# Window attention and a two-layer network on one core: value loads released one tile ahead of key and query loads, attention blocks moved among the products

## The chip, the cores and the metric

The kernel runs on one core of one Trainium2 chip. The core has five engines with instruction queues of their own: PE (TensorE, matrix products), DVE (VectorE), ACT (ScalarE), POOL (GpSimd) and SP (SyncE, which here only issues DMAs). Each executes its own queue in order; engines wait for each other, and for DMAs, through semaphores. The metric is the device time of one execution in microseconds. A profiled execution gives a span (first to last instruction) besides.

## The reference

Attention with a window of 128 positions and 4 sink positions, over q, k, v of shape (4 batches, 8 heads, 768 positions, 64); the heads are then put side by side as x of shape (4, 768, 512), which passes through a normalisation, a layer to 2048 with ReLU, a layer back to 512, and a residual:

```python
scores = scale * np.matmul(q, k.transpose(0, 1, 3, 2))
keep = is_sink | in_window                 # position < 4, or 0 <= row - column < 128
scores = np.where(keep, scores, -1000000000.0)
a = np.exp(scores - np.max(scores, axis=-1, keepdims=True))
a = a / (np.sum(a, axis=-1, keepdims=True) + 1e-09)
x = np.matmul(a, v)                        # then heads to the last axis: (4, 768, 512)
xn = (x - mu) / np.sqrt(var + 1e-06) * g_ln
out = x + np.maximum(xn @ w_ch1, 0.0) @ w_ch2
```

Inputs and output are float32; products run in bf16.

## The kernel before

**Tiles and chunks.** 3072 rows are 24 tiles of 128 rows; two tiles are a chunk, so there are 12 chunks, three to a batch. Weights stay in SBUF. In names, a number after a letter group is a tile or a chunk: `sc16` is the score block of tile 16, `ph6_0` the first product of chunk 6.

**What happens to a chunk** from chunk 4 on (chunks 0 to 3 get their keys and queries transposed by TensorE instead):

1. POOL issues four loads of keys and queries (`kld`, `qld`, L722; float32 in memory, bf16 in SBUF, 128 KB each in bf16) and six or seven loads of values (`vld`, L664, into a ring of seven buffers `vn`). `load_m` cuts the values into half blocks, because the 64-row halves of the windows lie differently for heads 0 to 3 and 4 to 7.
2. SP issues a transposing DMA for each loaded half (`trk`, `trq`, L595), giving kT and qT.
3. `block(t)` makes one block of matmuls, `sc{t}`, that holds the values product of tile t−1 (L976, L983, L992: probabilities times values) and the scores of tile t (L1003), and for an even tile the sink scores of the chunk (L1011). ScalarE takes the exponential (`ex`, L1021), VectorE applies the band mask (`mk`, L1026).
4. VectorE divides the values product of tile t−1 by the sums (`rc` and `x`, L1044 and L1046, one for each half of the heads), takes mean and variance (`bn`, `ag`, L900 and L902); POOL takes the power −1/2 (`rs`, L910 and L911); VectorE makes the normalised tile (`xc`, L914); SP issues the transposing DMA `trx` into xnt (L595 again).
5. `mlp(c)` multiplies xnt of the chunk (both tiles) with the first weights in eight products `ph{c}_0` to `ph{c}_7` (L1062, eight matmuls of 128x256 each); ScalarE or VectorE takes the ReLU (`rl`, L1073 and L1075). The second layer is, for chunks 3 to 10, a product by seven half-size products `P1` to `P7` (L1113, eight matmuls each; `k1`, `k6`, `k5` and `o12` copy from PSUM, L1119; `o11`, `o22`, `o21` add, L1123); for the others it is sixteen matmuls of 128x512 for each tile (`pc`, L1167). The residual is added (`o`, L1150 or L1175), and SP issues the store (`st`).

While TensorE does the products of one chunk, it does the score blocks of the next chunk between them: of a chunk's two blocks, `sc{2c}` and `sc{2c+1}`, each stands at a place among the products of chunk c−1 or its predecessor.

**What sets the order.** Every operation is recorded with a priority, its engine or engines, a cost, and its dependencies. `Plan.run` plays them through a small cost model and writes out one order for each engine; that order is then fixed in the program. Operations with two possible engines (ReLUs, copies) go to the one that the plan finds first free. The priority of a block is `at(c, "blk") + step * i - lead`, so `step` is the distance in priority between a chunk's two blocks and `lead` how far ahead of the default a chunk's blocks stand (`PAR["lead"]`, the last entry holding for all chunks from 5 on). A DMA has a triple for the plan: time on the shared line, delay before, delay after. `SHARED` is the time until which the plan counts transfers of both kinds of queue as one line; after it, each kind counts as a line of its own. None of these figures is in the program; the order that they lead to is.

**The gates.** `gate(c)` and `gate_v(c)` add a dependency to a chunk's key and query loads and to its value loads: they wait for `rs` of an earlier tile. A transposition of queries also waits for `trx` of tile 2c−3. POOL and SP issue in order, so a load that waits holds up what stands behind it.

PSUM has eight banks: four in two `pair` buffers for scores, four `one` buffers for everything else (two halves of a values product, `ph`, `P`).

Of the kernel before, what the change touches and what calls it, by code (L numbers as in the profile page):

```python
# [65 lines left out]
class Plan:  # L66
# [4 lines left out]
    PE_DRAIN = 0.18  # L71
    SWITCH = 0.095
    LANES = 8
    SHARED = 62.0

    def __init__(self):
        self.ops = []
# [36 lines left out]
    def run(self):  # L114
# [8 lines left out]
        while ready:  # L123
# [4 lines left out]
            for o in ready:  # L128
                if "PE" in o.engs and o is not head and o.prio >= PAR["strict"]:
                    continue  # L130
# [43 lines left out]
            else:  # L174
                busy, first, last = o.dma
                q = "POOL" if e == "POOL" else "HW"
                at = max(st + occ + first, dma_free[q], dma_free["all"] if st < self.SHARED else 0.0) + busy
                dma_free[q] = dma_free["all"] = at
# [18 lines left out]
def pe(us):  # L197
    return {"PE": (us, us + Plan.PE_DRAIN)}
# [7 lines left out]
def dve(n, per=1.04):  # L206
    t = 0.067 + 0.001 * per * n
    return (t, t + 0.09)


def fix(occ, extra=0.09):
    return (occ, occ + extra)


SW = (0.9, 0.7, 0.9)
# [2 lines left out]
SW_W = (2.65, 0.7, 0.9)  # L218
HW_F = (0.8, 2.2, 0.5)
HW_S = (0.75, 0.8, 1.2)  # L220
HW_X = (1.0, -0.2, 0.6)
SW_2 = (0.65, 0.7, 0.9)
HW_T = (0.10, 0.8, 0.8)
SW_H = (0.45, 0.7, 0.9)
SW_Q = (0.25, 0.7, 0.9)

LOW, HIGH = 1e-9, 1e9
LAST_CUTS, LAST_ACT = (0, 320, 512), (3,)
# [2 lines left out]
NEVER = -1e9  # L231
BIG = 3.3e38

PAR = dict(strict=400.0, win=0.4, tr=-8.0, sc=-5.0, sc1=-2.0, av=2.0, blk=-8.0, step=8.0, trx=9.0, by_dma=4, x_by_dma=2,
           w1p=(1.6, 2.6, 2.7, 2.8), pm=3, w2p=(4.5, 4.51, 4.52, 4.53), apart=2, vs0=(2.0, 13.0), by_tile=0, vp=(0.0, 0.1, 2.0, 2.1, 4.55, 4.56), ld1=0.05, t0=0.8, warm=7.9, pm0=-40.0, w1g=17.0, gtt=1.25, seven=3, lead=(0, 0, 0, 2, 4, 6), w2t=-4.0, at7=(0.5, 1.5, 2.5, 3.5, 4.5, 6.5, 7.5))


def general(tc, nc, slots, pairs, ones, ident_f, ident, w1, w2, mhalf, g_s, g_r, q, k, v, out, scale):
# [133 lines left out]
def kernel(  # L372
# [24 lines left out]
    NC = B * RC  # L397
# [70 lines left out]
    def constant(name, eng, us, prio, emit, reads=(), **kw):  # L468
        return P.op(name, {eng: fix(us)}, prio, emit, reads=[Bc[r] for r in reads], **kw)

    V, G = nc.vector, nc.gpsimd
# [44 lines left out]
    def negs(e):  # L516
# [27 lines left out]
    for b in range(B):  # L544
        n_vs = 4 if b else H
        P.op(f"vs{b}", {"DVE": dve(260)} if b else {"POOL": (0.9, 1.0)}, PAR["vs0"][0] if b == 0 else 48.0 * b - 20, lambda e, b=b, n=n_vs: (V if b else G).tensor_tensor(
            vs[b], vc[:, b, :].unsqueeze(1).to_broadcast([128, n, 65]),
            (sel4 if b else sel).unsqueeze(2).to_broadcast([128, n, 65]), op=ALU.mult),
            reads=[Bc["vcd"], Bc["vc"], Bc["sel4" if b else "sel"]], writes=[Bvs[b]], nb=PAR["vs0"][1] if b == 0 else 40.0 * b)

# [7 lines left out]
    for c in range(4):  # L558
        for n in range(len(Bw1[c])):
# [3 lines left out]
                 writes=[Bw1[c][n]], dma=half_w if len(Bw1[c]) > 1 else SW_W)  # L563
    for c in range(4):
        P.op(f"w2ld{c}", {"POOL": (0.75, 0.8)}, PAR["w2p"][c], lambda e, c=c: G.dma_start(
            w2[c], moe_w_ch2[512 * c:512 * (c + 1), :].rearrange("(t p) n -> p t n", p=128)),
            writes=[Bw2[c]], dma=SW_W)
# [17 lines left out]
    rs_op, trx_op = {}, {}  # L585
    natf_users, natp_users = [], []

    def gate(c):
        return [rs_op[2 * c - (4 if c > 5 else 5)]] if PAR["by_dma"] < c < NC else []

    def gate_v(c):
        return [rs_op[2 * c - (3 if c == 5 else 4)]] if PAR["by_dma"] < c <= NC else []

    def dma_t(dst, src):
        nc.sync.dma_start_transpose(out=dst, in_=src)  # L595
# [54 lines left out]
    def load_m(t, prio):  # L650
# [12 lines left out]
        for i, (p0, n, hs, src) in enumerate(parts):  # L663
            P.op(f"vld{t}_{i}", {"POOL": (0.8, 0.85)}, prio + 0.001 * i, lambda e, p0=p0, n=n, hs=hs, src=src: G.dma_start(  # L664
                m.t[p0:p0 + n, hs, 0:64], src), writes=[m], dma=SW_H if n == 128 else SW_Q, after=list(ones_of.values()) + gate_v(t // 2))

# [5 lines left out]
    def chunk(c):  # L672
# [3 lines left out]
        if c < 2:  # L676
            kT_b[c], qT_b[c] = Buf(f"kT{c}", "kT"), Buf(f"qT{c}", "qT")
            if c == 0:
                nats = [Buf("kf", "natf"), Buf("qf", "natf")]
                for hh in range(2):  # L680
                    hs = slice(4 * hh, 4 * hh + 4)
                    for i, (x, T) in enumerate(((k, kT_b[c]), (q, qT_b[c]))):
                        nm, src, part = "kq"[i], nats[i], Buf(f"{'kq'[i]}l{hh}")
                        ap = x[b, hs, 0:256, :].rearrange("h (p i) d -> p h (i d)", i=2)
# [3 lines left out]
                        nat, pt, done = Buf(f"{nm}c{hh}", "natc"), Buf(f"pt{nm}{hh}", "one"), Buf(f"{nm}T0{hh}")  # L688
                        natf_users.append(P.op(f"cast{nm}{hh}", {"DVE": dve(512), "ACT": act(512)}, d + 0.01 * hh,
                             lambda e, nat=nat, src=src, hs=hs: (nc.scalar.copy if e == "ACT" else V.tensor_copy)(  # L690
                                 nat.t, src.t[:, hs].rearrange("p h i d -> p i h d")),
# [18 lines left out]
        else:  # L710
            both = []
            for nm, src, bT in (("k", k, kT_b), ("q", q, qT_b)):
                T = Buf(f"{nm}T{c}", nm + "T")
                bT[c] = T
                if c < PAR["by_dma"]:
                    both.append((nm, src, T, ld + (0.1 if nm == "q" else 0.0)))
                    continue
                for i in range(2):
                    nat = Buf(f"{nm}n{c}{i}", "nat")
                    ap = src[b, :, 256 * R + 128 * i:256 * R + 128 * (i + 1), :].rearrange("h p d -> p h d")  # L720
                    P.op(f"{nm}ld{c}{i}", {"POOL": (0.87, 0.9)}, ld + 0.01 * i + (0.1 if nm == "q" else 0.0),
                         lambda e, nat=nat, ap=ap: G.dma_start(nat.t, ap), writes=[nat], dma=SW, after=gate(c))  # L722
                    P.op(f"tr{nm}{c}{i}", {"SP": (1.2, 1.2)}, d + 0.01 * i, lambda e, T=T, nat=nat, i=i: dma_t(
                        T.t[:, :, 128 * i:128 * i + 128], nat.t.rearrange("p h d -> p (h d)")),
                        reads=[nat], writes=[T], dma=HW_X, after=[trx_op[2 * c - 3]] if c > PAR["by_dma"] and nm == "q" else [])
            if both:
# [170 lines left out]
    def normalise(c, i, d, st, x, xc):  # L897
# [25 lines left out]
        if c >= PAR["x_by_dma"]:  # L923
            trx_op[t] = P.op(f"trx{t}", {"SP": (1.2, 1.2)}, d + 0.5, lambda e: dma_t(xnt_b[c].t[:, :, 128 * i:128 * i + 128], xc.t),
                 reads=[xc], writes=[xnt_b[c]], dma=HW_X)
            return
# [257 lines left out]
    for c in range(NC):  # L1184
        chunk(c)
        if c < 2:
            attend_tile(2 * c)
            attend_tile(2 * c + 1)
        elif c < RC:
            attend(c)  # L1190
        else:
            block(2 * c)
            block(2 * c + 1)
# [5 lines left out]
    w2t = [[flat_f[0][:, m] for m in range(2)], [flat_f[1][:, m] for m in range(2)], flat_p[0:2], flat_p[2:4]]  # L1199
# [21 lines left out]
    def guard(e):  # L1221
# [92 lines left out]
```

## Time and profile before

| | |
|---|---|
| time, three runs | 212.18, 213.89 and 215.04 us; median 213.89 us |
| profiled execution, time | 212.65 us |
| its span | 211.1 us |
| TensorE busy in the span | 202.0 us |
| VectorE, ScalarE, POOL busy | 156.8, 116.0, 114.3 us |
| bytes moved by DMAs | 28.06 MB |
| queue of POOL's DMAs, queue of SP's DMAs: time of their packets, share of 16 engines' span | 91.3%, 38.1% |

Lines of the profile name the engine, the line of the kernel, the operation, what is written from what is read (buffer numbers left out), a count, busy or elapsed time, and the idle time of the engine just before with what ended it. Issuing a DMA is no busy time of SP; a DMA's issue and its landing are different moments. A wait for several semaphores is put down to the one that came last by the profile. PEclk, the clock granted to TensorE, is full speed in the whole span. The profile is of one execution.

### The profile page before, as it was taken

How to read it: one execution, taken by the hardware profiler on the slowest of the kernel's cores; microseconds unless marked ns; L12 is line 12 of the kernel's file. 1: busy time of each engine (PE TensorE's matmuls, PEld its weight loads, DVE VectorE, ACT ScalarE, POOL GpSimd, SP SyncE). 2: the span in 40 equal slices, each digit the busy share in tenths (PEclk: the TensorE clock that was granted, in tenths of full speed). 3: DMA queues.
4: the chain of work that ended last, by engine and by line, in shares of the span. 5: the costliest groups of instructions: out<-in, count | busy, mean ns of one | idle time of the engine just before them, and what ended most of it. 6: DMA issues, size and time to landing. Idle time of an engine off the chain costs nothing.

```text
span 211.1 us, 7043 instructions
## 1 busy us (share of the span) xinstructions
PE 202.0 (96%) x2891; PEld 161.2 (76%) x2891; DVE 156.8 (74%) x426; ACT 116.0 (55%) x200; POOL 114.3 (54%) x169
## 2 busy tenths in 40 slices
PE   7799999999989998998999999999999999999994
PEld 2458865755865887886888888887888888888853
DVE  5599877999766489789688799788797788891321
ACT  4798697285662473564474564563563563454510
POOL 7969842479837972981970991972961321030000
PEclk9999999999999999999999999999999999999999
DMA  5999999999999999999999799899999520310203
GB/s 158 188 187 200 190 207 198 171 174 143 151 198 162 132 145 133 82 148 187 82 142 181 66 169 180 90 147 169 115 200 89 112 56 1 127 26 3 99 0 109
DMA packets 105644, 28.06 MB, mean 133 GB/s; under 512 B 94852, under 2 KB 102664, under 8 KB 105608
## 3 DMA queue, kind: packets, MB, share of 16 engines
q0 software_dynamic: 70960, 13.18, 91.3%
q1 hardware_dynamic: 33448, 13.71, 38.1%
q10 hardware_dynamic: 1200, 0.69, 1.2%
q8 instruction: 23, 0.38, 0.7%
q14 instruction: 13, 0.11, 0.2%
HBM read 27.43 MB, written 6.29 MB: 160 GB/s over the span
## 4 chain that ended last, share of the span: by engine, by line
PE 74%; DMA 12%; DVE 9%; ACT 2%; POOL 1%; issue 1%; ACTq 0%; DVEq 0%
PE one L1062 33%; PE one L1113 17%; PE one L1167 13%; DMA xnt<-xc 6%; DMA qT<-nat 3%; DMA natf<-in_q_dram 3%; DVE st L900 2%; PE pair L1003 2%; PE one L976 2%; PE one L983 1%; DVE x L1046 1%; PE one L992 1%; PE pair L1011 1%; ACT qT L669 1%; POOL st L911 1%
## 5 line engine op out<-in xcount | busy, mean ns | idle before, releaser
L1062 PE MATMUL one<-xnt,w 128*128 128x256 bf16 x768 | 89.8, 273 | 2.1 <-DMA xnt<-xc 1.1
L1062 PEld LDWEIGHTS <-w 128*128 128x128 bf16 x768 | 73.5, 98 | 13.6 <-DMA xnt<-xc 2.3
L1073 ACT ACTIVATE h<-one 128x512 bf16<-128x512 f32 x87 | 52.0, 598 | 40.1 <-PE one L1062 39.0
L664 POOL DMA_DIRECT2D vn<-in_v_dram x59 | 39.4, 695 | 8.4 <-DMA w<-in_moe_w_ch_dram 7.1
L1021 ACT ACTIVATE pe<-pair 128x768 bf16<-128x768 f32 x36 | 27.3, 808 | 22.7 <-PE pair L1003 22.3
L910 POOL TENSOR_SCALAR st<-st 128x1 f32<-128x1 f32 x24 | 9.3, 388 | 56.0 <-DVE st L902 55.3
L1167 PE MATMUL one<-w,h 128*128 128x512 bf16 (+2 forms) x144 | 29.5, 356 | 0.1
L1167 PEld LDWEIGHTS <-h 128*128 128x128 bf16 x144 | 13.4, 98 | 12.3 <-DMA w<-in_moe_w_ch_dram 0.4
L1113 PEld LDWEIGHTS <-h 128*128 128x128 bf16 x192 | 18.8, 98 | 2.5 <-issue 0.2
L911 POOL TENSOR_TENSOR st<-st,mhalf 128x1 f32<-128x1 f32 x24 | 16.5, 688 | 2.0
L900 DVE BATCH_NORM_STATS2 st<-x 128x6 f32<-128x512 bf16 x24 | 16.6, 693 | 0.7
L1113 PE MATMUL one<-w,h 128*128 128x256 bf16 x128 | 16.6, 273 | 0.1
L1113 PEld LDWEIGHTS <-sb 128*128 128x128 bf16 x156 | 15.0, 98 | 1.9
L722 POOL DMA_DIRECT2D nat<-in_k_dram x16 | 15.0, 938 | 2.2 <-DMA natp<-in_q_dram 1.5
L1046 DVE TENSOR_TENSOR x<-one,rec 128x256 bf16<-128x256 f32 x36 | 15.2, 422 | 0.9
L1123 DVE TENSOR_TENSOR ot<-one,tx 128x256 f32<-128x256 f32 x24 | 9.5, 420 | 7.5 <-PE one L1113 4.9
L1175 DVE SCALAR_TENSOR_TENSOR ot<-one,st,x 128x512 f32<-128x512 f32 (+2 forms) x9 | 6.2, 691 | 11.6 <-PE one L1167 10.3
L1119 ACT COPY tx<-one 128x256 f32<-128x256 f32 x17 | 6.3, 372 | 14.7 <-PE one L1113 14.7
L722 POOL DMA_DIRECT2D nat<-in_q_dram x16 | 14.4, 912 | 0.0
L1150 DVE TENSOR_TENSOR ot<-ot,x 128x512 f32<-128x512 f32 x16 | 11.1, 692 | 3.1 <-ACT ot L1119 2.7
L914 DVE TENSOR_SCALAR xc<-x,st 128x512 bf16<-128x512 bf16 x16 | 6.6, 413 | 7.3 <-POOL st L911 7.0
L1026 DVE TENSOR_TENSOR pe<-pe,band 128x768 bf16<-128x768 bf16 x24 | 12.0, 540 | 0.0
(145 smaller groups left out, 294.6 us busy)
## 6 DMA issues: line engine op xcount, KB each, us to landing
out_dram<-ot SPq DMA_DIRECT2D x23, 256.0 KB
w<-in_moe_w_ch_dram POOLq DMA_DIRECT2D x6, 512.0 KB, 10.8
nat<-in_k_dram POOLq DMA_DIRECT2D x16, 128.0 KB, 4.7
nat<-in_q_dram POOLq DMA_DIRECT2D x16, 128.0 KB, 7.0
vn<-in_v_dram POOLq DMA_DIRECT2D x44, 32.0 KB, 6.1
w<-in_moe_w_ch_dram POOLq DMA_DIRECT2D x4, 256.0 KB, 11.9
vn<-in_v_dram POOLq DMA_DIRECT2D x15, 64.0 KB, 7.2
natp<-in_k_dram POOLq DMA_DIRECT2D x3, 256.0 KB, 12.2
```

The costliest lines, as they stand in the source:

```text
L664: P.op(f"vld{t}_{i}", {"POOL": (0.8, 0.85)}, prio + 0.001 * i, lambda e, p0=p0, n=n, hs=hs, src=src: G.dma_start(m.t[p0:p0 + n, hs, 0:64], ...
L722: lambda e, nat=nat, ap=ap: G.dma_start(nat.t, ap), writes=[nat], dma=SW, after=gate(c))
L900: P.op(f"bn{t}", {"DVE": fix(0.60)}, d + 0.12, lambda e: V.bn_stats(st.t[:, 8:14], x.t), reads=[x], writes=[st, mv])
L911: G.tensor_tensor(st.t[:, 16:17], st.t[:, 17:18], mhalf, op=ALU.pow)),
L1021: nc.scalar.activation(pes[j].t.rearrange("p a b -> p (a b)")[:, 0:768].rearrange("p (a b) -> p a b", a=2), pps[j].t[:, :, 0:384], AF.Exp, ...
L1026: V.tensor_mul(at_s, at_s, band[j] if r > 1 else edge[r][j].unsqueeze(1).to_broadcast([128, 4, 192]))
L1046: P.op(f"x{t - 1}{u}", {"DVE": dve(256)}, d + 0.051 + 0.002 * u, lambda e, u=u, rc=rc, pv=pv: V.tensor_tensor(x.t[:, 256 * u:256 * u + 256 ...
L1062: nc.tensor.matmul(ph.t[:, 256 * s:256 * s + 256], lhsT=w1[ht // 4][:, j, 128 * (ht % 4):128 * (ht % 4 + 1)], rhs=xnt.t[:, j, :], start=j ...
L1073: nc.scalar.activation(dst, ph.t, AF.Relu)
L1113: nc.tensor.matmul(bank.t[:, 0:256], lhsT=left[p](m)[:, a, :], rhs=right[p](m)[:, a, :], start=new and m + a == 0, stop=m + a == 4, skip_g ...
L1150: V if e == "DVE" else G).tensor_tensor(ot[i].t, ot[i].t, x.t, op=ALU.add), reads=[ot[i], *oo[i], x], writes=[done])
L1167: nc.tensor.matmul(pc.t[:, 0:wd], lhsT=h1[s].t[:, 256 * ii + 128 * i:256 * ii + 128 * i + 128], rhs=w2[s][:, ii, sl], start=ht == 0, stop= ...
```

## The change

Value loads of chunk c get their dependency from `rs` of tile 2c−5 in place of 2c−4 (for chunk 5, of tile 6 in place of 7); the key and query loads keep theirs (`rs` of 2c−4, for chunk 5 of 2c−5 = 5). Attention blocks get a `step` of 10 in place of 8 and, from chunk 5 on, a lead of 9 in place of 6, so the first block of such a chunk has a priority 3 steps, and the second 1 step, further ahead; for chunks 3 and 4 the second block's is 2 steps further back. The plan counts one line for all DMAs to the end, and costs of four kinds of transfer in the plan are altered: the transposing DMA, the loads of keys and queries (which get a triple of their own, `SW_N`) and the two kinds of value loads. No operation is added or taken away; the order on each engine, and the engine of some copies and ReLUs, follow from the plan.

```diff
-    SHARED = 62.0
+    SHARED = 1000.0
...
-HW_X = (1.0, -0.2, 0.6)
-SW_2 = (0.65, 0.7, 0.9)
+HW_X = (0.75, 0.2, 1.2)
+SW_N = (1.05, 0.8, 1.4)
 HW_T = (0.10, 0.8, 0.8)
-SW_H = (0.45, 0.7, 0.9)
-SW_Q = (0.25, 0.7, 0.9)
+SW_H = (0.5, 0.7, 0.9)
+SW_Q = (0.28, 0.7, 0.9)
...
-PAR = dict(strict=400.0, ..., step=8.0, ..., lead=(0, 0, 0, 2, 4, 6), ...)
+PAR = dict(gk=(5, 4), gv=(4, 5), strict=400.0, ..., step=10.0, ..., lead=(0, 0, 0, 2, 4, 9), ...)
...
     def gate(c):
-        return [rs_op[2 * c - (4 if c > 5 else 5)]] if PAR["by_dma"] < c < NC else []
+        return [rs_op[2 * c - PAR['gk'][c > 5]]] if PAR["by_dma"] < c < NC else []
 
     def gate_v(c):
-        return [rs_op[2 * c - (3 if c == 5 else 4)]] if PAR["by_dma"] < c <= NC else []
+        return [rs_op[2 * c - PAR['gv'][c != 5]]] if PAR["by_dma"] < c <= NC else []
...
-                         lambda e, nat=nat, ap=ap: G.dma_start(nat.t, ap), writes=[nat], dma=SW, after=gate(c))
+                         lambda e, nat=nat, ap=ap: G.dma_start(nat.t, ap), writes=[nat], dma=SW_N, after=gate(c))
```

In the order that results, on TensorE (chunk 5's products and the blocks of tiles 15 and 16 as an example; before, then after):

```
ph5_7 P1_5 P7_5 sc15 P6_5 P2_5 P5_5 ph6_0 P3_5 ph6_1 P4_5 sc16 ph6_2
ph5_7 P1_5 sc15 P7_5 P6_5 P2_5 P5_5 ph6_0 P3_5 sc16 P4_5 ph6_1 ph6_2
```

and on POOL (the loads of chunks 8 and 9 between the statistics of tiles 11 to 14):

```
rs12 kld8 x2 qld8 x2 vld16 x3 vld17 x1 rs13 vld17 x2 rs14 kld9 x2 qld9 x2 ...
rs11 vld16 x3 vld17 x3 rs12 kld8 x2 qld8 x2 rs13 vld18 x4 vld19 x3 rs14 kld9 x2 qld9 x2 ...
```

More of the change, by code (lines that the diff above doesn't have):

```diff
@@ L232 @@
 BIG = 3.3e38
-PAR = dict(strict=400.0, win=0.4, tr=-8.0, sc=-5.0, sc1=-2.0, av=2.0, blk=-8.0, step=8.0, trx=9.0, by_dma=4, x_by_dma=2,
-           w1p=(1.6, 2.6, 2.7, 2.8), pm=3, w2p=(4.5, 4.51, 4.52, 4.53), apart=2, vs0=(2.0, 13.0), by_tile=0, vp=(0.0, 0.1, 2.0, 2.1, 4.55, 4.56), ld1=0.05, t0=0.8, warm=7.9, pm0=-40.0, w1g=17.0, gtt=1.25, seven=3, lead=(0, 0, 0, 2, 4, 6), w2t=-4.0, at7=(0.5, 1.5, 2.5, 3.5, 4.5, 6.5, 7.5))
+PAR = dict(gk=(5, 4), gv=(4, 5), strict=400.0, win=0.4, tr=-8.0, sc=-5.0, sc1=-2.0, av=2.0, blk=-8.0, step=10.0, trx=9.0, by_dma=4, x_by_dma=2,
+           w1p=(1.6, 2.6, 2.7, 2.8), pm=3, w2p=(4.5, 4.51, 4.52, 4.53), apart=2, vs0=(2.0, 13.0), by_tile=0, vp=(0.0, 0.1, 2.0, 2.1, 4.55, 4.56), ld1=0.05, t0=0.8, warm=7.9, pm0=-40.0, w1g=17.0, gtt=1.25, seven=3, lead=(0, 0, 0, 2, 4, 9), w2t=-4.0, at7=(0.5, 1.5, 2.5, 3.5, 4.5, 6.5, 7.5))
 def general(tc, nc, slots, pairs, ones, ident_f, ident, w1, w2, mhalf, g_s, g_r, q, k, v, out, scale):
```

## The prediction

> **What bounds the kernel now.** I read the busy shares first, then what TensorE waits for, then its timeline, then the two queues that feed it (SP and POOL).
>
> From the page, the busy row:
>
> ```profile
> PE 202.0 (96%) x2891; PEld 161.2 (76%) x2891; DVE 156.8 (74%) x426; ACT 116.0 (55%) x200; POOL 114.3 (54%) x169
> ```
>
> TensorE has 9.1 us without work in a span of 211.1 us. The change touches nothing ahead of tile 6 and nothing in the last block, so the idle time that it can reach lies between. The timeline of TensorE shows it in the brackets (start, length, group, then idle time before and its releaser):
>
> ```profile
> 60.31 0.29 PE L1011 MATMUL pair<-qT,kts 128*32 128x128 bf16 x8 [0.72 <-DMA qT<-nat]
> ...
> 69.39 2.78 PE L1062 MATMUL one<-xnt,w 128*128 128x256 bf16 x24
> ...
> 84.03 1.03 PE L1062 MATMUL one<-xnt,w 128*128 128x256 bf16 x8 [0.55 <-DVE pe L1026]
> ...
> 100.10 1.05 PE L1062 MATMUL one<-xnt,w 128*128 128x256 bf16 x8 [0.81 <-DMA xnt<-xc]
> ...
> 135.65 0.24 PE L1011 MATMUL pair<-qT,kts 128*32 128x64 bf16 x8
> ...
> 146.98 1.05 PE L1062 MATMUL one<-xnt,w 128*128 128x256 bf16 x8 [0.44 <-DVE pe L1026]
> ...
> 162.85 1.05 PE L1062 MATMUL one<-xnt,w 128*128 128x256 bf16 x8 [0.24 <-DMA xnt<-xc]
> ```
>
> The five waits add to 0.72 + 0.55 + 0.81 + 0.44 + 0.24 = **2.76 us**, and that is nearly all there is to gain: 1.3% of the span. One is the sink scores of tile 8, waiting for the transposed queries of chunk 4. The other four are the first product of a chunk's first layer (ph4_0, ph5_0, ph8_0, ph9_0), which needs both halves of the normalised, transposed activations xnt. Two of the four carry a VectorE name, but this matmul reads no masked scores; the queue of SP shows what else it waits for:
>
> ```profile
> 63.30 2.01 SPq L595 DMA_TRANSPOSE xnt<-xc  x1
> ...
> 78.17 1.22 SPq L595 DMA_TRANSPOSE xnt<-xc  x1
> ...
> 93.93 1.20 SPq L595 DMA_TRANSPOSE xnt<-xc  x1
> 95.23 2.83 SPq L595 DMA_TRANSPOSE qT<-nat  x2
> ...
> 129.39 1.22 SPq L595 DMA_TRANSPOSE qT<-nat  x1
> ```
>
> The second xnt half of ph4_0 is issued at 78.17, 5.86 us before the product starts. For the wait at 100.10, which does carry its name, the same distance is 100.10 − 93.93 = 6.17 us, and the chain of waits gives the queries of chunk 4 as much (start, length):
>
> ```profile
> 53.80 6.46 DMA qT<-nat
> ...
> 85.06 0.87 PE one L1113 x8
> ```
>
> So I read all four as the landing of a transposition, some 6 us after its issue. The second row is the unit of the sums below: one block of eight matmuls, a **slot**, is 0.87 us.
>
> Why 6 us: ahead of the issue at 93.93, POOL has put out four key and query loads and a first part of six V loads (timeline of POOL):
>
> ```profile
> 85.15 1.87 POOL L722 DMA_DIRECT2D nat<-in_k_dram  x2 [0.34 <-issue]
> 86.99 1.78 POOL L722 DMA_DIRECT2D nat<-in_q_dram  x2
> 88.72 2.78 POOL L664 DMA_DIRECT2D vn<-in_v_dram  x4
> ...
> 99.38 0.43 POOL L910 TENSOR_SCALAR st<-st 128x1 f32<-128x1 f32 x1 [5.06 <-DVE st L902]
> ```
>
> and V loads themselves land late in that crowd, but not in the emptier stretch after 62 us (the view of tile vn, for 62 to 67 and for 88 to 95 us):
>
> ```profile
> L664 POOL DMA_DIRECT2D vn<-in_v_dram x6: 626/656/842, 62.8 to 66.2; - x6
> DMA to landing us min/median/max: 3.9/4.1/4.4
> ```
>
> ```profile
> L664 POOL DMA_DIRECT2D vn<-in_v_dram x6: 630/685/817, 88.7 to 93.7; - x6
> DMA to landing us min/median/max: 6.2/6.5/7.7
> ```
>
> **The change part by part.** *The plan's constants* (shared line, costs of loads and transposes) issue nothing; they and the new lead and step change the order that is written out. The built order has the same matmuls and moves whole blocks. sc7 goes one slot later; sc8, sc9 and sc10 two later. sc11 and each later odd block go one slot earlier (between P1 and P7). sc12 keeps its distance from the next chunk's ph_0, sc14 goes one slot earlier, and the even ones from sc16 on two (right behind P3). Moving a block among slots costs TensorE nothing in itself; what counts is whether its inputs and the next chunk's are there.
>
> *V loads.* From chunk 5 on a chunk's V loads stand ahead of its key and query loads on POOL, behind the statistics of one tile earlier. The number of loads is the same. The wait is for the POOL instructions just in front, so nothing queues behind it in vain. Behind the six issues (6 × 0.69 = 4.1 us) stand the next tile's statistics; POOL waited 5.06 us for those in the row at 99.38, so 4.1 us fit. The slots of the ring of seven that they fill were last read by the block whose statistics release them, or an earlier one, so no load waits for a slot. Cost: nothing; if the 5.06 us were gone, each xnt would be later by what is left of 4.1.
>
> *VectorE and ScalarE.* The plan now hands the k6 copies and several ReLUs to ScalarE; VectorE has 13 operations fewer, ScalarE 12 more, POOL one (the residual of tile 18). At some 0.6 us each (L1073 on the page has 598 ns), ScalarE takes up 7 us more beside its 95 us of idle time. The POOL residual isn't shown by the trace of before: between nothing and, if the six V loads' 4.1 us are its ceiling, 4.1 us; behind it on POOL stands only the statistic of the last tile, which the last chunk's output reads at the end, so I take 0. The gain on VectorE is where it held x back, in tile 9:
>
> ```profile
> 73.03 0.42 DVE L1046 TENSOR_TENSOR x<-one,rec 128x256 bf16<-128x256 f32 x1
> 73.38 0.17 DVE L1044 RECIPROCAL rec<-one 128x4 f32<-128x4 f32 x1
> 74.37 0.69 DVE L1075 TENSOR_SCALAR h<-one 128x512 bf16<-128x512 f32 x1 [0.82 <-PE one L1062]
> 74.98 0.41 DVE L1046 TENSOR_TENSOR x<-one,rec 128x256 bf16<-128x256 f32 x1
> ```
>
> The second half waits for a ReLU between; without it, it could start near 73.55, 1.4 us earlier.
>
> Now the waits, one by one.
> - *sc8:* its sinks could start at 60.31 − 0.72 = 59.59, two slots later at 61.33. The queries landed at 53.80 + 6.46 = 60.26, 1.07 us before that; an output store now goes ahead of them on SP and may take some of the 1.07. The wait goes: −0.72. Bounds: −0.72 to 0.
> - *ph3_0, which had no wait:* TensorE reaches it at 69.39 − 0.72 = 68.67. The xnt half of tile 7 hangs on sc8 and moves with it, from 63.30 to 65.04. It has 3.63 us to land, where it had 6.09. This is a **new wait**: nothing if it lands within 3.63, 6.46 − 3.63 = 2.8 if it takes the longest above. The row for the same stretch (3.9 to 4.4) is the nearest, since chunk 5's V loads, then behind it, are now ahead and done: +0.27 to +0.77, and I take +0.5.
> - *ph4_0:* it had 84.03 − 0.55 − 78.17 = 5.31 us. sc10 two slots later takes 1.74, x without the ReLU gives 1.4: 4.97 us. Landing takes 5.86 in before's crowd, 3.9 to 4.4 without; chunk 6's V loads are long in. −0.55; bounds −0.55 to +0.34.
> - *ph5_0, ph8_0, ph9_0:* the xnt issue is held up on SP by the k transposes, whose loads hang on statistics of an odd block, now one slot (0.87 us) ahead. That alone exceeds 0.81, 0.44 and 0.24, even if landing still takes 6.17: −1.49; bounds −1.49 and 0.
>
> Sum: −2.76 + 0.5 = **−2.3 us**: span 208.8. The profiled run took 212.65 us around its span of 211.1, and is at the low side of the three runs (212.18 to 215.04, median 213.89); since the terms are differences, I take them from the median: **211.6 us**.
>
> [...]
>
> **The rivals.**
> 1. *The crowd is not the V loads (214.5).* If transposes land in some 6.1 us with or without V loads ahead, then ph3_0 waits 6.17 − 3.63 = 2.5 and ph4_0 5.86 − 4.97 = 0.9; the other four waits go by order alone. 213.89 − 2.76 + 2.5 + 0.9 = 214.5. For it: the key loads and output stores remain, and the transposition at 53.80 took 6.46 with other traffic as well. Against: 3.9 to 4.4 us in the stretch after 62.
> 2. *The queries come late (slower, 217.1).* V loads now go out beside the odd xnt and the two q transposes that follow it on SP, while the score block that reads them stands up to two slots earlier (one more than the k loads that precede them). In chunk 9 the second q issue ends at 130.61 and the sinks start at 135.65: 5.04 us, less one slot 4.17. In chunk 7 the pair ends at 98.06:
>
> ```profile
> 104.65 0.29 PE L1011 MATMUL pair<-qT,kts 128*32 128x128 bf16 x8
> ```
>
> that is 6.59, less one slot 5.72. If landing after the issue takes the longest V time less an issue, 7.7 − 1.2 = 6.5, chunk 9 waits 2.3 and chunk 7 0.8; with 8, 10 and 11 like 7, 5.5 in all: 213.89 − 2.3 + 5.5 = 217.1. It begins to cost above 4.17 us. Against: V loads stood ahead of these transposes before too, all six of them, and none of these sinks waited.
> 3. *V loads don't move:* excluded, they stand ahead in the built order.
>
> **How the numbers follow.** Forecast 0.62 (own range 210.2 to 213.2: the bounds of ph3_0 and 0.8 us of drift of a median of such runs), rival 1 0.20, rival 2 0.12, anything else 0.06. The range goes from 209.9, all 2.76 us and as much luck with the median as the forecast allows, to 215.4, with rival 1 and the drift in and most of rival 2 out. Two per cent, about what a measurement of this kernel can tell from no change, is 4.3 us. All waits together are 2.76, so faster by more takes a lucky median: 0.06. Slower by more takes rival 2 beyond its price: 0.06. Within: 0.88.
>
> **What would show it.** In the new trace: no idle time ahead of the sinks of tile 8 and ahead of ph5_0, ph8_0, ph9_0; some 0.5 us ahead of ph3_0 near 68.7; landing of V loads at about 4 us where it was 6.5; TensorE busy for the same 202 us. I am wrong if ph3_0 or ph4_0 waits 2 us (rival 1), if L1011 or L1003 waits for qT from chunk 7 on (rival 2), or if a block now waits for a PSUM bank: sc16 and its like take the bank of ph_0 one slot after it was filled, and its ReLU of 598 ns leaves 0.1 us there.

## The result, and the profile after

The changed kernel takes **211.90 us** (median of 20 runs, 210.96 to 212.83). The kernel before took 215.17 us beside it (20 runs with the three shown, 212.18 to 220.0). The ratio is 0.9908, with a 95% interval from 0.988 to 0.9936: a gain of 0.9%, less than the 2% that counted as faster. Ratios leave out executions over 1.5% above the fastest of their kernel; before has many such, after none, and the last section says what is known of them. The profiled execution took 211.49 us around a span of 210.0, where before it was 212.65 around 211.1.

The page's busy row after the change:

```profile
PE 201.6 (96%) x2891; PEld 161.7 (77%) x2891; DVE 151.7 (72%) x413; ACT 121.4 (58%) x212; POOL 115.9 (55%) x170
```

TensorE has the same matmuls and nearly the same busy time (202.0 before), so the difference lies in its waits. Its timeline at the places the prediction spoke of (start, length, group, in brackets the idle time before and its releaser):

```profile
17.43 0.28 PE L1062 MATMUL one<-xnt,w 128*128 128x256 bf16 x1
...
61.97 0.29 PE L1011 MATMUL pair<-qT,kts 128*32 128x128 bf16 x8 [0.66 <-DMA qT<-nat]
...
70.11 4.53 PE L1062 MATMUL one<-xnt,w 128*128 128x256 bf16 x40 [0.63 <-DMA xnt<-xc]
...
85.21 1.03 PE L1062 MATMUL one<-xnt,w 128*128 128x256 bf16 x8 [0.98 <-DMA xnt<-xc]
...
100.31 1.04 PE L1062 MATMUL one<-xnt,w 128*128 128x256 bf16 x8
...
146.30 1.04 PE L1062 MATMUL one<-xnt,w 128*128 128x256 bf16 x8
...
161.75 1.04 PE L1062 MATMUL one<-xnt,w 128*128 128x256 bf16 x8
...
177.20 0.38 PE L1062 MATMUL one<-xnt,w 128*128 128x256 bf16 x2
```

In order: ph0_0, the sinks of tile 8, ph3_0, ph4_0, ph5_0, ph8_0, ph9_0, ph10_0. From ph4_0 to ph10_0 no bracket is left; up to it there are three, 2.27 us in all, one more than before had there. Set against the starts of before, the change loses first and gains later. ph0_0 started at 17.15 before and starts at 17.43, ph4_0 at 84.03 and 85.21, ph10_0 at 178.31 and 177.20 (the first and last rows of before):

```profile
17.15 0.39 PE L1062 MATMUL one<-xnt,w 128*128 128x256 bf16 x2
...
178.31 0.38 PE L1062 MATMUL one<-xnt,w 128*128 128x256 bf16 x2
```

That is +0.9 us from ph0_0 to ph4_0 and −2.29 from ph4_0 to ph10_0 (94.28 to 91.99). From ph10_0 to the end both take 32.8 us.

The queue of SP (upper three rows) and the timeline of POOL (lower three) after the change:

```profile
65.03 1.19 SPq L595 DMA_TRANSPOSE xnt<-xc  x1
...
79.37 1.22 SPq L595 DMA_TRANSPOSE xnt<-xc  x1
...
93.82 1.20 SPq L595 DMA_TRANSPOSE xnt<-xc  x1
```

```profile
64.51 3.91 POOL L664 DMA_DIRECT2D vn<-in_v_dram  x6
...
78.73 4.06 POOL L664 DMA_DIRECT2D vn<-in_v_dram  x6
...
99.32 0.43 POOL L910 TENSOR_SCALAR st<-st 128x1 f32<-128x1 f32 x1 [1.94 <-DVE st L902]
```

POOL had 5.06 us to spare ahead of the statistic in the last row, and has 1.94 with the six V loads in front: they fit, as forecast. But their issue now starts 0.5 to 0.6 us ahead of the transposition of each odd tile (64.51 and 65.03, 78.73 and 79.37). They are no longer ahead of it; they are beside it.

In the later stretch V loads land sooner, though in this execution not at the forecast 4 us; in the earlier one they do not (the view of tile vn, 62 to 67 and 88 to 100 us; before, the medians were 4.1 and 6.5):

```profile
L664 POOL DMA_DIRECT2D vn<-in_v_dram x4: 620/636/695, 64.5 to 66.4; - x4
...
DMA to landing us min/median/max: 4.0/4.5/5.0
```

```profile
L664 POOL DMA_DIRECT2D vn<-in_v_dram x6: 638/668/842, 93.3 to 96.7; - x6
...
DMA to landing us min/median/max: 4.4/5.6/6.0
```

### The profile page after: what moved, and what is told of

Read it like the earlier page. It is cut to its first block, busy times and chain, and to the rows that moved or that the text cites. A ratio compares the mean times of both kernels' runs of the same rounds, so it can differ in the third digit from the quotient of the medians.

```text
span 210.0 us, 7046 instructions
## 1 busy us (share of the span) xinstructions
PE 201.6 (96%) x2891; PEld 161.7 (77%) x2891; DVE 151.7 (72%) x413; ACT 121.4 (58%) x212; POOL 115.9 (55%) x170
## 3 DMA queue, kind: packets, MB, share of 16 engines
HBM read 27.43 MB, written 6.29 MB: 161 GB/s over the span
## 4 chain that ended last, share of the span: by engine, by line
PE 81%; DMA 11%; DVE 4%; ACT 1%; issue 1%; POOL 1%; ACTq 0%; DVEq 0%; POOLq 0%
PE one L1062 37%; PE one L1113 22%; PE one L1167 11%; DMA xnt<-xc 5%; DMA qT<-nat 4%; DMA natf<-in_q_dram 3%; PE pair L1003 2%; PE one L976 2%; PE one L983 1%; PE one L992 1%; DVE st L900 1%; PE pair L1011 1%; DVE x L892 1%; PE pair L623 1%; PE pair L749 1%
## 5 line engine op out<-in xcount | busy, mean ns | idle before, releaser
L1062 PE MATMUL one<-xnt,w 128*128 128x256 bf16 x768 | 88.4, 273 | 1.6 <-DMA xnt<-xc 1.6
L1073 ACT ACTIVATE h<-one 128x512 bf16<-128x512 f32 x92 | 54.8, 599 | 37.2 <-PE one L1062 36.0
L910 POOL TENSOR_SCALAR st<-st 128x1 f32<-128x1 f32 x24 | 9.8, 410 | 49.4 <-DVE st L902 48.9
L1119 ACT COPY tx<-one 128x256 f32<-128x256 f32 x24 | 8.9, 372 | 18.4 <-PE one L1113 18.4
L1150 DVE TENSOR_TENSOR ot<-ot,x 128x512 f32<-128x512 f32 x15 | 10.4, 692 | 7.2 <-ACT ot L1119 7.0
```

What stands on the lines that cost most here:

```text
L1062: nc.tensor.matmul(ph.t[:, 256 * s:256 * s + 256], lhsT=w1[ht // 4][:, j, 128 * (ht % 4):128 * (ht % 4 + 1)], rhs=xnt.t[:, j, :], start=j ...
L1073: nc.scalar.activation(dst, ph.t, AF.Relu)
L1150: V if e == "DVE" else G).tensor_tensor(ot[i].t, ot[i].t, x.t, op=ALU.add), reads=[ot[i], *oo[i], x], writes=[done])
```

## The experiments

The diff changes an order, so each experiment but the repeats and the pauses is a kernel in which the order of every engine is written down as a list (in place of the plan's choice) and only the entries named are moved. **A** is the theory that the blocks' order did the work, **B** that the V loads' place did.

| run | what it is | median us (runs) | ratio to before, 95% interval | waits in the profiled execution, us |
|---|---|---|---|---|
| x1_v_only | before, V loads early | 211.32 (10) | 0.9959, 0.990 to 1.001 | 1.36 |
| x2_order_only | after, V loads where before had them | 213.96 (10) | 1.0027, 0.998 to 1.007 | 3.89 |
| x3_early_kept | after, order of before up to tile 11's block | 211.96 (10) | 0.9943, 0.988 to 1.000 | 1.71 |
| x5_v_stores | x1, two stores moved on SP | 212.00 (12) | 0.9918, 0.987 to 0.997 | 3.13 |
| x6_stores | after, two stores moved on SP | 212.42 (12) | 0.9932, 0.987 to 0.999 | 3.90 |
| a2_after | after again | 211.89 (6) | 0.9898, 0.982 to 0.998 | 2.56 |
| x9_early_v67 | a mixture, below | 211.06 (6) | 0.9861, 0.982 to 0.990 | 1.54 |
| x10_v_from8 | a mixture, below | 210.49 (6) | 0.9841, 0.979 to 0.989 | 1.21 |
| a3_after | after again, beside x10 | 211.29 (6) | 0.9885, 0.984 to 0.993 | 0.96 |

Before measured 214.68 beside x1 to x3, 214.96 beside x5, x6 and a2, 214.39 beside x9, 213.84 beside x10 and a3. The last column adds brackets of 0.1 us and more between 55 and 180 us, without those put down to "issue" (0.16 us each). x4, x7 and x8 stand below; they were run one, one and four times.

**Which half of the change works: x1 and x2.** x1 is before with the new dependency of V loads and their new place on POOL, nothing else; x2 is after with the old dependency.

```diff
 # x1
-        return [rs_op[2 * c - (3 if c == 5 else 4)]] if PAR["by_dma"] < c <= NC else []
+        return [rs_op[2 * c - (4 if c == 5 else 5)]] if PAR["by_dma"] < c <= NC else []
 # x2
-PAR = dict(gk=(5, 4), gv=(4, 5), ...
+PAR = dict(gk=(5, 4), gv=(3, 4), ...
```

> Only the V loads' place on POOL is that of the changed kernel; every other engine keeps the order of before. Theory A (the gain after 86 us comes from the order of the blocks, which brings each xnt half to SP sooner): the waits before ph5_0, ph8_0 and ph9_0 stay, 1.0 to 1.5 us together, span 210.5 to 211.3. Theory B (it comes from V loads that no longer stand ahead of xnt in the DMA queues): they fall below 0.3 us together and ph4_0's 0.55 shrinks too, span 208.8 to 209.5.

> All engines have the order of the changed kernel, but the V loads stand where before had them, behind the key and query loads. Theory A: no waits before ph5_0 to ph9_0, span within 0.4 us of the changed kernel's 210.0. Theory B: waits of 1 us or more together return there, span 211 to 212, no faster than before.

TensorE's waits in x1, and then in x2:

```profile
60.76 0.29 PE L1011 MATMUL pair<-qT,kts 128*32 128x128 bf16 x8 [1.13 <-DMA qT<-nat]
...
130.52 1.03 PE L1062 MATMUL one<-xnt,w 128*128 128x256 bf16 x8 [0.23 <-DMA xnt<-xc]
```

```profile
84.54 1.03 PE L1062 MATMUL one<-xnt,w 128*128 128x256 bf16 x8 [1.08 <-DMA xnt<-xc]
...
100.66 1.05 PE L1062 MATMUL one<-xnt,w 128*128 128x256 bf16 x8 [0.86 <-DMA xnt<-xc]
...
130.41 0.61 PE L1113 MATMUL one<-natf,sb 128*128 128x256 bf16 x4 [0.86 <-DVE sb L1090]
```

With the V loads early and nothing else, ph4_0, ph5_0, ph8_0 and ph9_0 wait for nothing, and the time is that of after (a wait of 0.23 at ph7_0 is new). With the order alone, ph8_0 and ph9_0 are free too, but ph5_0 waits as before (0.81 then) and ph4_0 longer, and a new wait appears at 130.41. The chain of waits of x2 names that one: VectorE stood idle for 2.06 us, until 129.06, for a k transposition issued at 120.82, and the sums for the next product stood behind it in VectorE's order.

```profile
120.82 8.24 DMA kT<-nat
```

B holds: the gain is the V loads' place. x1 and x2 ran side by side, and the slowest of x1's ten executions (213.22) is faster than the fastest of x2's (213.41). Against before alone, x1's interval just includes no change. The moved blocks, the ReLUs moved to ScalarE and the plan's constants add nothing that can be measured (x1 211.32, after 211.9), and without early V loads they gain nothing clear of the noise (x2 213.96 beside 214.68). Theory B had the size of x2's waits and only in part their places: ph5_0 waits 0.86 us and the products at 130 us 1.26, while ph8_0 and ph9_0 are free.

**What the crowd costs: x4 and x7.** Both leave loads out, so values products read what the buffers hold: x4 is before without V loads from tile 12 on, x7 is after without those of tiles 12 to 15.

```diff
-                m.t[p0:p0 + n, hs, 0:64], src), writes=[m], ...
+                m.t[p0:p0 + n, hs, 0:64], src) if t < 12 else None, writes=[m], ...                   # x4
+                m.t[p0:p0 + n, hs, 0:64], src) if t not in (12, 13, 14, 15) else None, writes=[m], ... # x7
```

> The kernel before without its V loads from tile 12 on (the values products read what the buffers held); all orders else as before. It prices the crowd. Theory A: the second xnt half still lands 5.5 us or more after its issue and the waits before ph5_0, ph8_0, ph9_0 keep at least half of their 1.49 us. Theory B: it lands in 4 us or less, no waits from ph4_0 on, span 208.5 to 209.

> After without the value loads of tiles 12 to 15 (left out; the values products of those tiles read what the buffers hold). The four or five value loads issued ahead of the xnt half of tile 7 remain (tiles 10 and 11); the six issued right beside and behind it are gone, and so are those beside the xnt half of tile 9. Theory 'loads that start beside or behind a transposition delay it as well as those ahead': tile 9's half, 5.70 us from issue to landing in after, takes 4.0 to 4.6 and the wait ahead of ph4_0 goes (0.98 to 0); tile 7's, 4.95, takes 4.0 to 4.5 and the wait ahead of ph3_0 falls below 0.2. Theory 'only what is ahead in the queues counts': both keep their landing within 0.4 us and both waits stay above 0.5.

x4 (one run, 211.49 us; the order is that of before) has these two waits left, and none for xnt from ph4_0 on. Its span of 210.0 us misses the 208.5 to 209 expected, of which the wait ahead of the sinks, 1.69 where before had 0.72, makes up 1.0:

```profile
61.46 0.30 PE L1011 MATMUL pair<-qT,kts 128*32 128x128 bf16 x8 [1.69 <-DMA qT<-nat]
...
101.92 1.03 PE L1062 MATMUL one<-xnt,w 128*128 128x256 bf16 x8 [0.37 <-DVE ot L1123]
```

By the last packets in the traces, the second xnt half of chunks 4, 5, 8 and 9 took 5.7, 6.1, 6.2 and 6.6 us from issue to landing before, and 4.4, 3.4, 2.5 and 3.8 in x4: V loads add 1.3 to 3.7 us, by one execution of each. x7 (one run, 210.73 us) shows that this holds for loads beside the transposition too. Its SP and TensorE rows for ph4_0:

```profile
79.88 2.20 SPq L595 DMA_TRANSPOSE xnt<-xc  x1
```

```profile
83.88 1.04 PE L1062 MATMUL one<-xnt,w 128*128 128x256 bf16 x8
```

ph4_0 starts 4.0 us after the issue with no wait (the half landed after 3.34 us), where in after it waited until 85.21 − 79.37 = 5.84. In the eight profiles with chunk 7's V loads beside it this half took 4.79 to 5.78 us to land; with none, 4.4 in x4 and 3.34 here. In before, with four of chunk 6's loads ahead of it (from 72.76) and three beside it (from 77.64), it took 5.72: the change put one crowd in place of another there and left this landing as long as it was (5.71). ph3_0's wait is gone as well (3.95 us instead of 4.95), but a repeat of after with all its loads had 4.05 there, so that place alone would prove nothing.

**The early chunks: x3, and the stores in x5 and x6.** x3 is after with every engine in before's order up to the block of tile 11, V loads early. x5 and x6 are x1 and after with the stores of tiles 2 and 3 moved on SP:

```diff
 # x3, on PE (the other engines likewise)
-ph2_6 ph2_7 pc40_0 sc8 pc40_1 pc40_2 pc40_3 pc50_0 pc50_1 sc9 pc50_2 pc50_3 ph3_0 ph3_1 ph3_2 ph3_3 ph3_4 sc10 ph3_5
+ph2_6 sc8 ph2_7 pc40_0 pc40_1 pc40_2 pc40_3 sc9 pc50_0 pc50_1 pc50_2 pc50_3 ph3_0 ph3_1 ph3_2 sc10 ph3_3 ph3_4 ph3_5
 # x5 and x6, on SP
-trk40 st20 trk41 trq40 st30 trq41 trx6     # after (x1: trk40 st20 trk41 trq40 trq41 st30 trx6)
+trk40 trk41 trq40 trq41 st20 st30 trx6     # x6 and x5
```

> The changed kernel with the blocks sc7 to sc10 at the places that before had (two slots earlier for sc8 to sc10), V loads released early throughout. If the two slots are what makes ph3_0 wait 0.63 and ph4_0 0.98 us: ph3_0 under 0.2, ph4_0 under 0.4, sc8's wait for qT 0.5 to 0.8, no waits from ph5_0 on, span 208.3 to 208.9. If these waits come from the V loads of chunks 5 and 6, now ahead of xnt of tiles 7 and 9: both stay above 0.5, span 209.5 to 210.

> The order of before with the value loads early, and besides the stores of tiles 2 and 3 on SP behind the four transpositions of chunk 4 instead of one of them between the k transpositions. The second query transposition of chunk 4 is then issued 0.65 us earlier. Theory 'SP's issue order sets the wait ahead of the sinks of tile 8': that wait falls from 1.13 to about 0.5, and the time from 211.3 by 0.3 to 0.7 us to about 210.8; no other wait changes by more than 0.3. Theory 'the landing is set by the traffic, not by the moment of issue': the wait stays at 0.7 to 1.1 and the time at 211.3.

> After, with the stores of tiles 2 and 3 on SP behind the four transpositions of chunk 4 (two stores leave their place ahead of the last query transposition, 1.2 us). Theory 'two waits in a row share one price': the wait ahead of the sinks of tile 8 falls from 0.66 to 0, but the xnt half of tile 7 hangs on the part of that block ahead of the sinks and on POOL, so it lands where it did, near 70.0, and the wait ahead of ph3_0 grows from 0.63 to about 1.3; the time stays at 211.9. Theory 'each wait costs its own': ph3_0 stays at 0.6 and the time falls by 0.7 to 211.2.

> After itself once more, beside the others on the same chip: 211.9 us, and in its profile the waits ahead of the sinks of tile 8, ph3_0 and ph4_0 again, 2.3 us together; if these are chance of one execution, they stand elsewhere or differ by more than 0.5 us each.

x3, x5, x6 and a2, the waits from the sinks of tile 8 to ph4_0, a fence for each:

```profile
71.29 2.78 PE L1062 MATMUL one<-xnt,w 128*128 128x256 bf16 x24 [0.86 <-DMA xnt<-xc]
```

```profile
59.92 0.30 PE L1011 MATMUL pair<-qT,kts 128*32 128x128 bf16 x8 [0.20 <-DMA qT<-nat]
...
69.86 2.78 PE L1062 MATMUL one<-xnt,w 128*128 128x256 bf16 x24 [0.69 <-DMA xnt<-xc]
```

```profile
71.41 6.20 PE L1062 MATMUL one<-xnt,w 128*128 128x256 bf16 x40 [2.48 <-DMA xnt<-xc]
...
87.89 1.03 PE L1062 MATMUL one<-xnt,w 128*128 128x256 bf16 x8 [0.70 <-DMA xnt<-xc]
```

```profile
70.70 4.53 PE L1062 MATMUL one<-xnt,w 128*128 128x256 bf16 x40 [1.64 <-DVE ot L1175]
...
85.75 1.03 PE L1062 MATMUL one<-xnt,w 128*128 128x256 bf16 x8 [0.92 <-DMA xnt<-xc]
```

x3's order takes ph4_0's wait away (in this stretch one wait of 0.86 at ph3_0 instead of three), and the time stays at 211.96. So one half of its first expectation came, and the other, under 0.2 at ph3_0, did not; a wait of 0.55 at ph7_0 is new. The stores do set the issue of the last query transposition, and with them behind, its wait falls to 0.20 (x5) and to nothing (x6). But the time does not fall in either. In x6 the wait at ph3_0 is longer, and in a2, where the queries happened to land in time without any edit, it is 1.64: whoever saves 0.66 ahead of the sinks waits at ph3_0 instead, since the xnt half of tile 7 is issued no sooner: at 65.03 in after, with the wait ahead of the sinks, and at 65.20, 65.04 and 65.20 in a2, a3 and x6, without it. (The row of a2 names VectorE, but the half landed at 70.57, 0.13 us ahead of the start.) Two waits in a row share one price. Which of the two shows is chance of the execution, and the size hangs on the landing: ph3_0's wait was 0.63, 1.64 and 0.47 in the three profiles of after (after, a2, a3), where the half took 4.95, 5.37 and 4.05 us. x6's 2.48 is more than the 1.3 expected, because the half took 6.07 us to land instead of 4.95; x5's execution had a wait of 2.24 at ph5_0 that x1 had not. Both executions are special in one more way, which the pauses below take up.

**A better version: x9, x10 and a3.** Both are after with before's order up to the block of tile 11 and the stores as in x6. In x9 the V loads of chunks 6 and 7 stand where before had them; in x10 those of chunk 5 as well.

```diff
-        return [rs_op[2 * c - PAR['gv'][c != 5]]] ...
+        return [rs_op[2 * c - (4 if c in (6, 7) else PAR['gv'][c != 5])]] ...                 # x9
+        return [rs_op[2 * c - ((4, 3)[c == 5] if c < 8 else PAR['gv'][c != 5])]] ...          # x10
```

> After, but the blocks of tiles 7 to 10 where before had them, the stores of tiles 2 and 3 behind chunk 4's transpositions, and the value loads of chunks 6 and 7 at the places of before (value loads of chunk 5 and from chunk 8 on early). Theory 'loads beside the transposition set each landing': the xnt half of tile 7 lands within 4.3 us and ph3_0 does not wait, the sinks of tile 8 wait 0.3 or less, ph4_0 waits 0.3 to 0.7 (value loads of chunk 6 stand ahead of tile 9's half, as in before), ph5_0 0 to 0.5; waits in all about 1.0 where after has 2.3, and a time of about 210.8. If it is at 211.5 or more, the loads put off at one place are paid for at the next, and nothing is to be gained by where they stand.

> As the run with the places of before for the value loads of chunks 6 and 7, and chunk 5's too (behind the statistics of tile 7, so that they are issued beside the xnt half of tile 7 and not ahead of it): value loads early from chunk 8 on alone. Theory 'what is ahead weighs more than what is beside': tile 7's half lands 0.5 to 1.5 us sooner after its issue than 5.85, ph3_0's wait of 0.52 goes, the others stay (0.4 each) and the time is 210.5. Theory 'ahead and beside weigh the same': ph3_0 waits 0.3 to 0.8 and the time is 211.1.

> After itself, on the same chip as the run before it: 211.9 us. If the version beside it is within 0.3% of it, the gain of 0.8 us seen for its like was chance.

The two differ in one thing around the xnt half of tile 7 (issued at 63.44 and 63.69): chunk 5's V loads are put out from 57.6 on in x9, and from 63.17 on in x10. POOL's DMA queue in the view of DMAs for 63 to 65 us (packets, MB, time of packets as a share of 16 engines), x9 and then x10:

```profile
q0 software_dynamic: 1418, 0.17, 170.0%
```

```profile
q0 software_dynamic: 47, 0.01, 25.7%
```

and TensorE at ph3_0, x9 and then x10 with its only wait of the stretch, ph4_0:

```profile
69.42 2.78 PE L1062 MATMUL one<-xnt,w 128*128 128x256 bf16 x24 [0.52 <-DMA xnt<-xc]
```

```profile
68.98 1.26 PE L1062 MATMUL one<-xnt,w 128*128 128x256 bf16 x10
...
84.30 1.03 PE L1062 MATMUL one<-xnt,w 128*128 128x256 bf16 x8 [1.21 <-DMA xnt<-xc]
```

The half lands 3.57 us after its issue in x10 and 5.85 in x9: in this pair, loads ahead cost more than loads put out at the same moment. It is also where x9's theory failed: with no V loads issued beside it, the half was to land within 4.3 us and ph3_0 not to wait. But x7 has the same six loads ahead, put out from 57.55 on, and none beside, with the half issued 1.9 us later, and there it took 3.95. Over all profiles with chunk 5's V loads ahead, this landing took 3.95 to 6.29 us (ten, mean 5.4); with them beside, 3.57 to 5.22 (four, mean 4.4). Eight of the ten have chunk 6's loads beside it as well, and the spans overlap, so that loads ahead cost more than loads beside is not shown. x10's ph4_0 waits 1.21 where 0.4 was expected. x10 is 0.8 us below after on the same chip, 210.49 against 211.29; by the means of six runs each it is 0.7 us, with a 95% interval of about 0 to 1.4. It is the best version found, some 0.3% below after, at the edge of what the runs can tell.

**Pauses: x8.** The executions of x5 and x6 that were profiled had a stretch at half clock (a mean of 0.52 over 3.5 us) right behind their longest wait (2.24 and 2.48 us). x8 is after with a pause of its own ahead of ph7_0, ph8_0, ph9_0 and ph10_0: an additional matmul waits for POOL, which adds up the copy of the product before.

```diff
+                dl and not u and nc.tensor.matmul(ph.t[:, 0:256], lhsT=w1[0][:, 0, 0:128], rhs=dl_t, start=True, stop=False, ...)
+DOSES = {7: [], 8: [128], 9: [256], 10: [256, 256]}
+        for n in DOSES[c]:
+            G.tensor_tensor(dl_f[:, 0:n], src[:, 0:n], src[:, 0:n], op=ALU.add)
+        G.tensor_tensor(dl_t[:, 0:256], src[:, 0:256], src[:, 0:256], op=ALU.add)
```

> After with a pause put ahead of ph7_0, ph8_0, ph9_0 and ph10_0: each waits for one, two, two and three additions on POOL that read the copy of the product just before (128x256 each, in the second pause one of 128x128 and one of 128x256). From the one POOL addition in the profile of after (1.15 us for 128x512) I estimate pauses of about 1.5, 2.0, 2.3 and 3.0 us. Theory 'a pause of TensorE above some 2 us halves its clock for 3.4 us': the granted clock falls to half once behind the two or three longer pauses and not behind the first; each fall costs 1.7 us beside its pause, so the time is 211.9 + 8.8 + 3.4 to 5.1, that is 224 to 226 us. Theory 'the falls seen so far came by chance or from the traffic': the clock stays at full speed behind all four, and the time is 211.9 + 8.8, some 221 us.

```profile
132.47 0.27 PE L1058 MATMUL one<-dl_t,w 128*128 128x256 bf16 x1 [1.21 <-POOL dl_t L1505]
149.40 0.27 PE L1058 MATMUL one<-dl_t,w 128*128 128x256 bf16 x1 [1.56 <-POOL dl_t L1505]
166.92 0.27 PE L1058 MATMUL one<-dl_t,w 128*128 128x256 bf16 x1 [1.80 <-POOL dl_t L1505]
185.12 0.27 PE L1058 MATMUL one<-dl_t,w 128*128 128x256 bf16 x1 [2.49 <-POOL dl_t L1505]
```

and the granted clock on x8's page, in 40 slices of 5.5 us:

```profile
PEclk9999999999999999999999999999999999799999
```

The pauses came out shorter than estimated, and only the last, 2.49 us, is followed by a fall of the clock (the 7, the slice from 186.7 to 192.2 us). The median is 221.47 us (4 runs). Three of the four executions have a mean granted clock of 0.991 or 0.992, at 221.12 to 222.62 us; the fourth, at 0.999, took 220.28 us. So neither expectation was right in its number: the time is near that of the second, but a fall of the clock is there, behind the pause of 2.49 us and not behind those of 1.21, 1.56 and 1.80. With the pauses as they came out (7.06 us together) and one fall at 1.7, the first theory gives 211.9 + 7.1 + 1.7 = 220.7 us; the profiled execution took 221.12.

## Why the prediction was right, and where it was wrong

The forecast case came about and its number, 211.6, is 0.3 us from the median. The mechanism is right, that transpositions land sooner when V loads are out of their way (1.3 to 3.7 us sooner in x4), but the close number is in part luck. In the two profiled executions the terms come to 0.5 us and not to the 2.3 of the sum, and two errors cancelled at ph3_0. The base, a median of three runs, was 1.3 us below that of twenty.

- **What bounds the kernel:** right. As far as the brackets show, all that changed is waits of TensorE for transpositions. ph4_0's wait carried a VectorE name before and carries xnt's now, at the same distance from the issue (5.86 then, 5.84 now): it was the landing.
- **Price of a wait:** it costs some 0.16 us more than its bracket says, where it can be read off. Before ph5_0 the last full product started at 98.25, 1.85 us ahead; without a wait the same step is 0.88 (99.43 to 100.31 in after):

```profile
98.25 0.60 PE L1113 MATMUL one<-natf,sb 128*128 128x256 bf16 x4
```

```profile
99.43 0.60 PE L1113 MATMUL one<-natf,sb 128*128 128x256 bf16 x4
```

  That is 0.97 us lost where the bracket has 0.81. A landing can also cost without any bracket: from ph6_0 to ph7_0 before took 15.72 us and after 15.45. So 2.76 us was not "nearly all there is to gain".
- **V loads cost POOL nothing:** right (1.94 us still to spare). **Copies and ReLUs to ScalarE:** free, right: VectorE fell by 5.1 us and ScalarE rose by 5.4 with no wait behind it. The gain expected from them in tile 9 did not come to the end either: x1, without them, has the same time.
- **sc8, −0.72:** wrong in this profile (0.66 left). The failing step is the margin of 1.07 us: one of the two stores now goes between the query transpositions, the last is issued at 54.52 instead of 53.80, 0.72 us later, was under way 0.95 us longer, and landed at 61.93 instead of 60.26. In the two repeats the wait was under 0.1, in x7 and x8, with the same order up to there, 1.25 and 0.33. But the term is empty either way: without the wait here TensorE only comes sooner to ph3_0, whose xnt half is issued no sooner.
- **ph3_0, +0.5:** the new wait is there, 0.63 here and 0.47 and 1.64 in repeats, and its cause, the later issue, was right (65.03, forecast 65.04). The size is luck. TensorE came to ph3_0 at 70.11 − 0.63 = 69.48 and not at 68.67, since the sinks still waited, so the half had 4.45 us to land and not 3.63; and it took 4.95, where 3.9 to 4.4 was taken. That price is the landing of V loads; this transposition itself had taken 5.21 us in before.
- **ph4_0, −0.55, at most +0.34:** wrong, by the most: the wait grew to 0.98. The time allowed was right: 85.21 − 0.98 − 79.37 = 4.86 us (forecast 4.97). The landing was not: 5.71 us where 3.9 to 4.4 was taken. The failing words are "chunk 6's V loads are long in": they are, but chunk 7's six, released one tile earlier like all others, now start at 78.73, beside this very transposition. x7 takes them out, with chunk 6's, and the landing falls to 3.34 and the wait goes. The prediction followed the V loads out of one stretch and not into the next.
- **ph5_0, ph8_0, ph9_0, −1.49:** right in the result, half wrong in the reason. "That alone exceeds", it said of the order, "even if landing still takes 6.17". For ph8_0 and ph9_0 that holds (x2). For ph5_0 it does not: with the order alone the half took 7.42 us to land and the wait was 0.86. And x1 takes all three away without the order. Early V loads do not make ph5_0 safe in every execution either: x5, with them, waited 2.24 us there, and its half took 7.2 us.
- **The basis:** the terms add up to −2.27 + 2.76 = 0.5 us less waiting in these two executions (with 0.16 more for each wait, an estimate from the one that could be read off, about 0.8), the spans differ by 1.1 us, and the medians by 3.3. The profiled execution of before was a good one. At full clock the two kernels differ by 2.1 us (last section), near the forecast 2.3, so the sum fits a usual execution better than the pair that was profiled. What I read from it: before's waits vary from execution to execution, since in its profile the halves of all six chunks 4 to 9 landed within 0.14 us of their product's start, waiting or not, so any slower landing is a wait; from ph5_0 on the changed kernel has 1.4 to 4.6 us in hand. Its runs spread over 1.9 us, those of before over 7.8.
- **Rival 1** (the crowd is not the V loads) is refuted by x1, x4 and x7. Its 0.9 us at ph4_0 came true all the same, through V loads. **Rival 2** (late queries) did not come: no wait for qT behind 62 us in after. Whether V loads **ahead of a transposition or beside it** cost more, the runs settle only in part: without the loads of chunks 6 and 7, six of them beside it, the transposition for ph4_0 landed 2.4 us sooner (x7, 3.34 against 5.71). Moving loads from ahead of tile 7's half to beside it took off 2.3 us in one pair (5.85 in x9, 3.57 in x10), but in x7, with six loads ahead, it took 3.95, so that may be chance, and which of the two costs more is open.
- No block waited for a PSUM bank: between 86 and 180 us after has no bracket of TensorE at all. The 0.1 us that the prediction leaves there does not follow from the figures it shows, 0.87 − 0.598 = 0.27.

## What to carry to other kernels

When a load is moved out of the way of a transfer, follow it to where it goes, and list every transfer that it now starts beside: here the same move took the waits from three products (ph5_0, ph8_0, ph9_0) and put six other loads beside a fourth's transposition, whose landing stayed as long as it was. Before counting a wait as gained, ask which wait behind it depends on something that doesn't move; the two share one price. Give a gain against a kernel whose margins are near zero from many executions, since one profile may show its best.

## What the runs showed of the hardware

**The three waits of 2.24 to 2.49 us cost a second time, through the clock.** TensorE's granted clock around the wait of x6, by windows (us, then busy time of PE, PEld, DVE, ACT and POOL, then the granted clock, DMA share and GB/s):

```profile
69.00:71.40 2.40, 0.00 (x0) 0.02 (x1) 1.81 (x4) 0.00 (x0) 2.30 (x4) 1.00 1.87 191
71.40:72.00 0.60, 0.59 (x6) 0.54 (x7) 0.00 (x0) 0.00 (x0) 0.60 (x1) 0.98 1.63 240
72.00:75.50 3.50, 3.50 (x20) 2.51 (x18) 0.38 (x1) 1.19 (x2) 2.58 (x4) 0.52 1.80 156
75.50:79.00 3.50, 3.50 (x91) 3.05 (x89) 1.17 (x5) 2.32 (x4) 0.00 (x0) 1.00 2.35 191
```

Here the clock falls 0.6 us after the wait of 2.48 us has ended, and stays at half for some 3.4 us: 20 matmuls stand in a window of 3.5 us that holds 91 afterwards (smaller ones in part), and 3.5 × 0.48 = 1.7 us are lost beside the wait, by this estimate. The same followed the 2.24 us in x5 (0.52 from 102.0 to 105.5 us) and the 2.49 us in x8 (0.52 from 185.7 to 189.2), and no wait of 1.13 to 1.80 us in any profile. In the traces of x6 and x8 the clock changes at 71.98 and 75.39 us and at 185.68 and 189.09, each time a whole multiple of 3.41 us behind its first record (7.13 and 4.77). There is one fall without such a wait: in x3's execution the clock stood at half from 9.52 to 12.93 us, in the start-up, where the longest bracket behind 2 us is 0.83. So the figures above are of waits among dense products (2.24 us and more with a fall, 1.80 and less without), and what brings a fall in the start-up is open. So is why one of x8's four executions kept its clock (mean 0.999): no trace shows that one's pauses.

**Many executions of before have a low mean clock.** One fall makes a mean of 0.992 (x5, x6 and x8). Of the 70 executions of before that ran beside the experiments, 26 have a mean granted clock of 0.992 or less, with a median of 216.2 us; the other 44 have a median of 213.9. Of after's 32 executions none has (median 211.8). Early V loads alone do not prevent it: x3 has two in ten, x5 two in twelve and x6, after with two stores moved, four in twelve. Comparing executions at full clock, the change is worth 2.1 us; comparing all, 2.9 (medians 214.7 and 211.8). Twenty of after's 32 ran at another time than the 70; beside a2 and a3, at full clock, it is 2.1 and 2.4. That before's falls stand behind long waits for transpositions is what its margins suggest, but it was not shown: its only profile has none, and x3's lies in the start-up.

**Landings vary.** The same transposition in the same order (tile 7's in after) took 4.95, 5.37 and 4.05 us to land in three executions. A margin below 1 us is no margin here.
